# Tile 1's q and k over SyncE's ring with GpSimd casts, so that GpSimd's ring starts with the weights, and a new cost model in the planner

**Chip, cores, metric.** One core of one Trainium2 chip. The metric is device time in microseconds (us), lower is better; a time is the median of several runs. All times compared below are of undisturbed runs; the few runs that came in the second, slower state (over 1.5% above the fastest: four of the kernel before, one of before_tail3) are left out. They still spread: the 39 undisturbed runs of before, on several chips, go from 238.07 to 240.68 us. Times inside a trace count from the start of its span.

## What is computed

```python
# q, k, v: (4, 8, 768, 64); is_retrieval: 8 flags; n_sink 4; window 64
scores = np.matmul(q, k.transpose(0, 1, 3, 2)) / 8
mask   = causal for flagged heads, else causal & (sink | in_window)
a      = softmax(where(mask, scores, -1e9))
x      = np.matmul(a, v) -> (3072 tokens, 512)
h      = x @ w_in              # 512 x 2048
g      = h - np.tanh(h)
out    = g @ w_out             # 2048 x 512, fp32
```

## The kernel before

The 3072 tokens go in 12 tiles of 256. For each tile the kernel makes scores, exp, the product with v, x, its transpose xT, the first layer (`ph`), g (`gt`) and the second layer (`po`). A planner, `Plan`, takes all operations with estimated costs, simulates five engines and two DMA rings, and emits the program in the order in which its simulated clock started them. Two facts matter below: the order on each engine is fixed at build time, so an engine waits in order; and a changed cost or load in the head shifts the simulated clock, and so can reorder **everything** after it.

```python
class Plan:
    ...
    def run(self):
        ...
            _, ns, _, _, dma, _, port, _ = self.ops[i]
            self.start[i] = t
            order.append(i)
            free[e] = t + max(ns - self.OVERLAP[e], 40)
            ...
            for u in followers[i]:
                ready[u] = max(ready[u], t + ns)
            ...
            if dma:
                packets, each = dma
                rings["POOL" if e == "POOL" else "SP"].append(
                    [i, t + ns + (1200 if e == "POOL" else 300), each, packets * each / 16]
                )
        ...
        for i in order:
            self.ops[i][2]()
...
        def paired(nm, t):              # q or k in runs of 512 B, two tokens of a head
            return nm != "v" and t == 0
        ...                             # other fp32 loads: runs of 256 B
        def load_cast(t, w_after=(), names="qkv"):
            ...                         # GpSimd's DMA reads fp32 and writes fp16: no cast needed
                        nc.gpsimd.dma_start(
                            out=o, in_=src[b, :, s0 : s0 + 128, :].rearrange("h p d -> p h d")
                        )
...
        for half in range(2):           # tile 0 over SyncE's ring, in halves of the heads
            load(0, "qk", (half,))
            load(0, "v", (half,))
...
        cast_qk(0, (("ACT", "ACT"), ("ACT", "DVE")), (0,))
        load_cast(1, [("rv", 0, "v", 0, 1)], "qk")     # tile 1: four casting loads on GpSimd's ring
        if first:
            load_w_in(*W_IN[0], ())                    # then the first quarter of w_in
            load_cast(1, (), "v")
        ...
        if first:
            load_w_in(*W_IN[1], ())
            load_w_in(*W_IN[2], ())
            scale_v(0, "POOL")
            load_w_in(*W_IN[3], ())
            load_w_out(0, ())
            ...                         # tile 2 and the other quarters of w_out
```

## Time and profile before

| | before |
|---|---|
| time, median of 3 | 238.31 us (238.22 to 238.36) |
| span of the profiled run | 236.7 us |
| first matmul, last matmul start | 6.01, 231.54 us |
| quarters of w_in land | 17.05, 23.67, 26.36, 28.98 us |
| quarters of w_out land | 31.41, 37.32, 41.70, 44.36 us |
| last store issued, landed, end of span | 232.36, 234.73, 236.74 us |

TensorE (PE) carries the kernel. A useful measure for it, worked out from the trace's matmul records, is the **loss by time T**: T less the work begun by then, where a matmul counts as the median distance to the next one of its kind (a 128-row, 256-column matmul of the first layer 0.109 us, one of 512 columns in the second 0.216 us, and so on). All kernels here do 205.6 us of such work. In before the loss is 15.9 us by 28, 19.5 by 60, 23.5 by 140 and 26.0 by 220: from 60 us to the end it still grows by 6.5. The prediction, which is quoted below, shows the other lines.

### The profile page before, as it was taken

What the parts mean: (1) busy time and instruction counts of PE and PEld (TensorE: products, weight loads), DVE (VectorE), ACT (ScalarE), POOL (GpSimd) and SP (SyncE); (2) the same over time, 40 slices, a digit from 0 to 9 for tenths busy, and PEclk for the clock granted to TensorE, in tenths of its full rate; (3) what the DMA queues carried; (4) which work ended last, traced back from release to release, by engine and by line L of the source; (5) the groups of instructions that cost most, each with busy time, mean ns of one, the idle gap of its engine ahead of it and who ended that gap; (6) DMA issues with size and microseconds to landing.
All of it is one profiled execution on the core that took longest, in us unless ns stands there. A gap on an engine that the chain in (4) does not pass through costs nothing. (4 is left out here: it accounts for less than half of the span.)

```text
span 236.7 us, 5895 instructions
## 1 busy us (share of the span) xinstructions
PE 221.5 (94%) x2220; PEld 157.8 (67%) x2220; DVE 139.0 (59%) x343; ACT 143.6 (61%) x221; POOL 90.5 (38%) x218
## 2 busy tenths in 40 slices
PE   0889899999999999999999999999999999999991
PEld 0346687756776777777676777776776777777661
DVE  1856665864488657767666655667766546443300
ACT  3668677884588387466686649537759464444320
POOL 5999420089818068480814904606300000000000
PEclk9999999999999999999999999999999999999999
DMA  5999999999997999979989695998712101310121
GB/s 128 209 140 172 204 181 204 197 228 224 206 225 182 151 248 184 227 153 206 239 168 214 136 186 130 186 171 179 134 47 66 38 31 47 90 38 9 44 89 51
DMA packets 108130, 35.29 MB, mean 149 GB/s; under 512 B 100290, under 2 KB 104642, under 8 KB 108098
## 3 DMA queue, kind: packets, MB, share of 16 engines
q1 hardware_dynamic: 92642, 28.98, 60.5%
q0 software_dynamic: 15168, 5.77, 20.7%
q8 instruction: 18, 0.29, 0.5%
q10 hardware_dynamic: 288, 0.14, 0.2%
q14 instruction: 14, 0.11, 0.2%
HBM read 27.27 MB, written 6.29 MB: 142 GB/s over the span
## 5 line engine op out<-in xcount | busy, mean ns | idle before, releaser
L1135 PE MATMUL ph<-xT,win 128*128 128x256 f16 x768 | 101.7, 273 | 0.6 <-DMA win<-in_moe_w_in_dram 0.3
L1194 PE MATMUL po<-wout,gt 128*128 128x512 f16 (+1 forms) x400 | 98.0, 371 | 0.3 <-ACT ot L1170 0.3
L1148 ACT ACTIVATE th<-ph 128x512 f32<-128x512 f32 x96 | 57.6, 601 | 59.6 <-PE ph L1135 58.2
L1155 DVE SCALAR_TENSOR_TENSOR gt<-th,ph 128x512 f16<-128x512 f32 x96 | 65.4, 684 | 44.9 <-ACT th L1148 44.4
L1135 PEld LDWEIGHTS <-win 128*128 128x128 f16 x768 | 80.0, 114 | 13.0 <-issue 1.9
L961 ACT ACTIVATE pt<-sc 128x1024 f16<-128x1024 f32 (+1 forms) x78 | 68.5, 926 | 11.4 <-PE sc L941 10.9
L1194 PEld LDWEIGHTS <-gt 128*128 128x128 f16 x400 | 36.4, 98 | 24.6 <-issue 0.9
L680 POOL CAST t<-raw_rqk 128x256 f16 x72 | 28.5, 440 | 63.3 <-DMA raw_rqk<-in_k_dram 48.1
L1030 PEld LDWEIGHTS <-pt 128*128 128x128 f16 x552 | 25.9, 98 | 10.4 <-issue 0.9
L1030 PE MATMUL av<-v,pt 128*128 128x65 f16 x304 | 26.0, 195 | 0.1
L941 PE MATMUL sc<-qk 64*128 64x128 f16 (+1 forms) x412 | 23.8, 240 | 1.7 <-DVE qk L826 1.7
L941 PEld LDWEIGHTS <-qk 64*128 64x128 f16 x412 | 13.7, 94 | 13.5 <-issue 8.9
L675 POOL CAST v<-raw_rv 128x128 f16 x72 | 21.1, 335 | 4.2 <-DMA raw_rv<-in_v_dram 4.2
L1060 DVE TENSOR_TENSOR x16t<-av,rinv 128x128 f32 x72 | 20.8, 289 | 2.3 <-DVE rinv L1050 0.3
L1030 PE MATMUL av<-vf,pt 128*128 128x65 f16 x248 | 19.6, 193 | 0.0
L1170 ACT ACTIVATE ot<-po 128x512 f32<-128x512 f32 (+1 forms) x24 | 14.3, 596 | 8.5 <-PE po L1194 8.4
L996 DVE TENSOR_TENSOR pt<-pt,m 128x1024 f16<-128x1024 f16 x16 | 12.3, 768 | 8.0 <-ACT pt L961 8.0
L1050 DVE RECIPROCAL rinv<-av 128x4 f32<-128x4 f32 x48 | 8.6, 179 | 13.4 <-PE av L1030 13.4
L986 DVE TENSOR_TENSOR pt<-pt,mS 128x512 f16<-128x512 f16 x24 | 9.8, 449 | 6.7 <-ACT pt L961 6.7
L843 PEld LDWEIGHTS <-t 128*128 128x128 f16 x48 | 3.9, 107 | 8.9 <-ACT t L644 6.8
L523 DVE TENSOR_SCALAR m<-A,thr 128x512 f16<-128x512 f16 x16 | 7.4, 501 | 1.7 <-PE sc L928 1.2
L751 POOL TENSOR_TENSOR vf<-v,rflagr 128x260 f16<-128x260 f16 x12 | 7.5, 634 | 0.0
(95 smaller groups left out, 90.8 us busy)
## 6 DMA issues: line engine op xcount, KB each, us to landing
out_dram<-ot SPq DMA_DIRECT2D x23, 256.0 KB, 2.3
raw_rqk<-in_q_dram SPq DMA_DIRECT2D x20, 256.0 KB, 4.7
raw_rqk<-in_k_dram SPq DMA_DIRECT2D x20, 256.0 KB, 4.5
raw_rv<-in_v_dram SPq DMA_DIRECT2D x18, 256.0 KB, 4.4
win<-in_moe_w_in_dram POOLq DMA_DIRECT2D x4, 512.0 KB, 8.8
wout<-in_moe_w_out_dram POOLq DMA_DIRECT2D x4, 512.0 KB, 12.4
raw_rv<-in_v_dram SPq DMA_DIRECT2D x4, 128.0 KB, 4.7
t<-in_q_dram POOLq DMA_DIRECT2D x4, 128.0 KB, 9.5
```

The costliest lines, as they stand in the source:

```text
L675: nc.gpsimd.tensor_copy(out=v1s[b]()[:, lo : lo + NB, rank : rank + 1, 0:D], in_=raw_of("v", t)[:, :, at, :],)
L680: nc.gpsimd.tensor_copy(out=t16[t % 2][:, :, :, rank : rank + 1, :], in_=raws["rqk", t][0]()[:, :, :, at, :],)
L941: nc.tensor.matmul(out=sc()[:, hh, o : o + nb * 128].rearrange("p (i c) -> p i c", c=128), lhsT=ks.rearrange("p i c -> p (i c)")[p_, jb * ...
L961: lambda pt=pt, gi=gi, wid=wid, sc=sc: nc.scalar.activation(out=pt()[:, :, 512 * gi : 512 * gi + wid], in_=sc()[:, :, 0:wid], func=AF.Exp, ...
L996: nc.vector.tensor_mul(out=pv, in0=pv, in1=m4[:, h0 : h0 + 2, 256:512].unsqueeze(2).to_broadcast([128, 2, 2, 256]),)
L1030: nc.tensor.matmul(out=av()[:, i, hh, :], lhsT=pt()[:, hh, co : co + 128], rhs=vv, start=(jb == first_jb), stop=(jb == qb),)
L1060: nc.vector.tensor_mul(out=x16s[t]()[:, :, at, :], in0=av()[:, :, hh : hh + 1, 0:D], in1=rinv()[:, :, hh : hh + 1].unsqueeze(3).to_broadca ...
L1135: nc.tensor.matmul(out=ph()[:, j, :], lhsT=w()[:, cb, c0 + fb % 4 : c0 + 512 : 4], rhs=xTs[t]()[:, cb, :], start=(cb == 0), stop=(cb == HP ...
L1148: lambda: nc.scalar.activation(out=th()[:], in_=ph()[:], func=AF.Tanh, scale=1.0 / XS),
L1155: lambda: nc.vector.scalar_tensor_tensor(out=gts[t]()[:, u * FU : (u + 1) * FU, :], in0=th()[:], scalar=-XS, in1=ph()[:], op0=ALU.mult, op ...
L1170: nc.scalar.activation(out=ot()[:, c0:c1], in_=po()[:, c0:c1], func=AF.Copy, scale=1.0 / XS)
L1194: nc.tensor.matmul(out=po()[:, c0:c1], lhsT=gts[t]()[:, f, ts * 128 : ts * 128 + 128], rhs=w_out_t[f // 4]()[:, f % 4, c0:c1], start=(f == ...
```

## The change

Intent: GpSimd's ring should have w_in sooner. So q and k of tile 1 move to SyncE's ring, uncast, in 512 B runs behind tile 0's data, and GpSimd casts them; its first DMA is now a quarter of w_in. The planner's cost model is also made to fit the chip: half clock for TensorE before 15 us, later landings of the first loads on SyncE's ring, and an issue that follows another on GpSimd's ring can be planned a little sooner.

```diff
@@ class Plan @@
-            if k[0] in self.PSUM:
+            if isinstance(k, tuple) and k[0] in self.PSUM:
@@
+            if e == "PE" and t < 15000:
+                ns *= 2
@@
-                ready[u] = max(ready[u], t + ns)
+                ready[u] = max(ready[u], free[e])
@@
-                    [i, t + ns + (1200 if e == "POOL" else 300), each, packets * each / 16]
+                    [i, t + ns + (1200 if e == "POOL" else 1000 if t < 6000 else 400), each, packets * each / 16]
@@
-            return nm != "v" and t == 0
+            return nm != "v" and t < 2 and (first or not t)
@@ the load of is_retrieval
-                "ACT", 400,
+                "ACT", 1150,
@@ (tile 0's six loads are written out in the order that the loop gave; not shown)
@@
         cast_qk(0, (("ACT", "ACT"), ("ACT", "DVE")), (0,))
-        load_cast(1, [("rv", 0, "v", 0, 1)], "qk")
         if first:
-            load_w_in(*W_IN[0], ())
+            load(1, "qk", (0,))
+            load(1, "qk", (1,))
+            cast_qk(1, (("POOL", "POOL"), ("POOL", "POOL")))
+        else:
+            load_cast(1, [("rv", 0, "v", 0, 1)], "qk")
+        cast_v(0, ("POOL", "POOL"), (0,))
+        cast_v(0, ("POOL", "POOL"), (1,))
+        if first:
+            load_w_in(*W_IN[0], raw_keys("q", 0, 1))
             load_cast(1, (), "v")
@@ (the two cast_v(0, ...) lines further down go; a list of first-layer transposes is kept and not used; not shown)
```

> **What bounds the kernel now.** I read the page's table of busy time and the slices first, then busy time by stretch, then the waits of TensorE, then the timeline of the stretches in which TensorE is not full, and last the landings of the head's DMAs.
>
> ```profile
> PE 221.5 (94%) x2220; PEld 157.8 (67%) x2220; DVE 139.0 (59%) x343; ACT 143.6 (61%) x221; POOL 90.5 (38%) x218
> ...
> 6.00:15.00 9.00, 8.12 (x56) 3.85 (x57) 6.21 (x16) 6.00 (x11) 8.77 (x12) 1.00 1.62 179
> 15.00:19.00 4.00, 3.00 (x43) 1.80 (x42) 3.23 (x12) 2.94 (x7) 4.00 (x6) 1.00 1.50 138
> 19.00:22.00 3.00, 3.00 (x38) 2.44 (x39) 1.36 (x4) 2.79 (x4) 3.00 (x4) 1.00 1.18 182
> 22.00:28.00 6.00, 4.78 (x59) 3.17 (x56) 4.25 (x11) 3.92 (x8) 3.79 (x5) 1.00 1.23 213
> 28.00:36.00 8.00, 7.97 (x98) 6.91 (x96) 5.01 (x11) 5.86 (x12) 1.97 (x3) 1.00 1.79 178
> 36.00:60.00 24.00, 23.05 (x267) 16.40 (x266) 14.69 (x49) 16.77 (x25) 11.57 (x30) 1.00 1.17 215
> 60.00:100.00 40.00, 39.73 (x435) 28.88 (x434) 28.26 (x68) 28.09 (x41) 21.64 (x57) 1.00 1.06 205
> 100.00:200.00 100.00, 100.00 (x1019) 71.75 (x1017) 63.50 (x151) 63.28 (x95) 32.71 (x91) 1.00 0.69 138
> ```
>
> The columns of a stretch are its bounds, its length, and busy time of PE, PEld, DVE, ACT and POOL. From 60 us on TensorE is all but full, so the kernel is bound by TensorE, and a change of the head is worth only what it lets TensorE do earlier. Before 60 us its idle time is 6.00 (nothing has landed and been cast), 0.88 in 6 to 15, 1.00 in 15 to 19, nil in 19 to 22, 1.22 in 22 to 28, 0.03 in 28 to 36 and 0.95 in 36 to 60: 4.1 us after its first matmul. The end (the last evacuation starts at 231.91, the span ends at 236.7) is not touched.
>
> Who ends these waits, and what stands around the longest two:
>
> ```profile
> PE xp L1108 <- DVE x L1074: 1.1, 3, 0.6
> PE sc L941 <- DVE qk L826: 0.7, 1, 0.7
> PE ph L1135 <- DMA win<-in_moe_w_in_dram: 0.3, 1, 0.3
> ...
> 15.20 0.28 PE L843 MATMUL tp4q<-ident,t 128*128 128x128 f16 x2
> 18.93 1.06 PE L1135 MATMUL ph<-xT,win 128*128 128x256 f16 x8
> 23.72 0.63 PE L1135 MATMUL ph<-xT,win 128*128 128x256 f16 x4 [0.30 <-DMA win<-in_moe_w_in_dram]
> 26.65 0.89 POOL L378 DMA_DIRECT2D v<-in_v_dram  x1 [1.75 <-DMA win<-in_moe_w_in_dram]
> 35.82 9.16 SPq L328 DMA_DIRECT2D raw_rqk<-in_k_dram  x2
> ```
>
> The first three are waits (us, times, longest), the others timeline rows (start, length). tp4q is the first work of tile 1; L1135 is the first layer on tile 0. The row at 23.72 is the key: the second quarter of w_in came just in time, 0.30 us late. Landing times of the trace say the same of the others: the quarters landed at 17.05, 23.67, 26.36 and 28.98, and L1135's groups on tile 0 start at 18.93, 20.69, 23.72, 25.37, 27.30 and 29.42. So in 22 to 28 us tile 0's first layer follows the arrival of weights, though only 0.3 us is booked as a wait for a DMA: a TensorE whose order was planned for these arrivals shows thin work, not one long wait. Counting columns at full clock (columns divided by 2.4, my reckoning), TensorE did 4.2 us of work in those 6 us, a loss of about 1.8. POOL, too, waits there for an old transfer to land before it may issue a new one.
>
> **What the skill says, and whether this trace agrees.** (1) TensorE: Matmul & The Clock Gate, Part 1, "What's actually happening": the array starts at half clock and is let go after a busy window of about 3.4 us. Agrees in kind: the clock's records start at 14.95 us, and a 128x128 transpose takes about 300 ns before and 219 after. So 6 to 15 us runs at half clock with TensorE 90% busy, and little can be pulled into it. (2) DMA: Bandwidth & Descriptors, "Queues, rings and completion order": the engines take packets in turn from the rings that have work. Agrees: in 39 to 41 us, when POOL's ring carried w_out and SP's the next q and k, the trace has 56 and 48 packets of the one against 55 and 48 of the other in each us; SP moved only 14 and 12 KB in them. (3) The same page, Specifications: 512 B are needed for line rate. The halves of q and k of tile 0, which go in such pairs, land some 0.95 us apart (256 KB each, 270 KB/us), and the casting loads of tile 1's q and k moved about 150 KB/us of half-size output, that is 300 KB/us read: here the longer packets gain nothing. (4) GPSIMD Engine Reference, 4.1: operations with one input run at about line rate. Agrees: a 128x512 cast took 0.61 us on POOL, 0.58 on DVE and 0.62 on ACT.
>
> **The change part by part.**
> Tile 0's six half loads keep their order on SP's ring; the rewritten calls list what the loop listed. First work stays at 6.0 us: nothing gained.
> Removed: four casting issues of q and k of tile 1 on POOL, 1.10 + 0.89 + 0.88 + 0.88 = 3.75 us of POOL. Added: four casts of 128x512 at 0.61, 2.44 us. POOL gains 1.3 us and is not the bound, so nothing by itself.
> Moved: the first w_in quarter goes first on POOL's ring, after the second half of tile 0's q has landed (8.28 before). I expect its issue at about 9.0 and its first packets about 1.5 us later (the first POOL issue ended at 7.19, its packets start near 8.7), at 10.5. Alone a quarter takes 2.65 us, the step between landings.
> Tile 1's four half loads: SP's data for tile 0 ends at about 9.3 (1.2 us ahead of the landing at 10.52). At 1.86 ns a packet (0.95 us for 512) one half and a quarter of the next are through by 10.5. Then packets alternate with w_in's at 5.2 ns each (2.65 us for 512), 7.1 a pair: the remaining 380 of k's first half take 2.7 us. Adding 1.2 to land, first halves come at about 11.4 (q) and 14.4 (k), second ones, beside the casting v loads, at about 16.4 and 17.9. With a cast of 0.61 the first k is ready at 15.0. Before, all landed by 13.53, yet their first transposes ran at 15.2 (q) and 17.7 (k), the second halves' at 22.0 and 23.1. So the later arrival is still in time.
> Weights: all bytes up to the second quarter are the same, only the order differs, but the hole in the DMAs at 13 to 14 us (65 KB moved, against some 200) goes, as does the stretch of POOL's late issues. From 9.3: q and k 3.8, first quarter 2.65, v 2.0, second 2.65, plus 1.2 to land: 21.6. I expect quarters at about 15.3, 21.6, 24.3 and 27.0: the last three some 2 us earlier.
> What TensorE makes of it. In 22 to 28 us I expect back 1.0 of the lost 1.8: the groups of L1135 no longer follow the weights, while the in-order wait for DVE's copy (0.7) may stay. In 15 to 19 I take 0.3 of 1.0, since the first layer still needs tile 0's xT, whose last copy starts at 18.62. That the order planner now counts TensorE's half clock and later first landings is of use there. In 36 to 60 I take 0.3 of 0.95, because w_out and tiles 2 and 3 follow on the same rings and shift too. Sum 1.6: 238.3 - 1.6 = 236.7.
>
> **Rivals.** (a) Weights starve tile 1: by the packet turns of (2), SP's ring gets about 100 KB/us beside w_in. If w_in starts before tile 1's first halves are through, k lands past 17, POOL waits in order in its cast and issues the next weights late. For it: the 9.16 us in which SP was held in two issues. Against it: SP's loads are issued first. It would give 238.5 to 240. (b) Nothing: in 15 to 28 us the chain from matmul to exp to mask to av to x to xT, and DVE's order, set the pace, and weights were only 0.3 us late. For it: the three waits on DVE, 1.8 us against 0.3. It would give 237.9 to 238.4. (c) More: a denser start frees the clock one window of 3.4 us sooner, which saves half of it, 1.7 us, beside the 1.6: 235. Against it: nothing of tile 0 comes earlier.
>
> **Range and chances.** The middle is between (b) and a full recovery of the 3.2 us idle in 15 to 19, 22 to 28 and 36 to 60, which gives 235.1. Rival (a) sets the upper side. I take 235.2 to 238.4 for 8 in 10. Faster by over 2% means below 233.5, which needs more than all the idle time there is after the first matmul: 0.02. Slower by over 2% means above 243.1, which needs a stall that nothing shows: 0.01. Within: 0.97.
>
> **What would show the steps.** Right: w_in's second quarter lands before 22.5; TensorE idles under 0.6 us in 22 to 28; no wait for DMA win; first matmul still at 6.0 and clock at 15; total of TensorE's busy time within 1.5 us of before. Wrong: POOL casts of tile 1 that wait long for DMA raw_rqk, or transposes of tile 1 later than 17.7 with TensorE idle before them (a); quarters 2 us earlier with L1135 no denser (b); the clock's record beginning near 11.5 (c).

## The result, and the profile after

| | before | after |
|---|---|---|
| time, median | 238.34 us of 4 (238.22 to 238.83) | 238.47 us of 4 (237.85 to 238.73) |
| ratio after to before | | 0.9998 (0.9974 to 1.0022): the same |

A ratio is the mean time of one kernel's fast runs over that of the other's in the same rounds, so not quite the ratio of the medians quoted.

By 60 us the head, in sum, did what was hoped. Busy time by stretch in after, columns as in the prediction (xN counts instructions; the last three numbers are the granted clock, the busy share of the DMA engines and GB/s):

```profile
15.00:19.00 4.00, 3.50 (x48) 2.01 (x45) 3.66 (x11) 3.28 (x6) 4.00 (x7) 1.00 1.72 191
...
22.00:28.00 6.00, 5.24 (x64) 3.82 (x65) 3.76 (x11) 3.65 (x7) 2.60 (x4) 1.00 1.26 205
28.00:36.00 8.00, 7.38 (x90) 5.58 (x90) 4.77 (x11) 6.07 (x13) 3.16 (x4) 1.00 1.86 182
36.00:60.00 24.00, 24.00 (x283) 18.32 (x281) 15.63 (x49) 17.51 (x27) 13.22 (x38) 1.00 1.10 221
60.00:100.00 40.00, 39.51 (x434) 28.34 (x429) 27.15 (x66) 27.40 (x41) 21.69 (x58) 1.00 1.10 197
100.00:200.00 100.00, 99.75 (x1010) 71.48 (x1009) 64.89 (x151) 62.74 (x94) 31.33 (x83) 1.00 0.67 137
```

TensorE is fuller than before in 15 to 19 (3.50 for 3.00), 22 to 28 (5.24 for 4.78) and 36 to 60 (24.00 for 23.05), but thinner in 28 to 36, and also in 60 to 100 and 100 to 200, where nothing was meant to change. The waits of TensorE in after (total, times, longest; the 6.0 us before the first work and three shorter ones are left out):

```profile
PE po L1200 <- DMA wout<-in_moe_w_out_dram: 0.6, 2, 0.4
PE tp6k L848 <- ACT qk L829: 0.5, 1, 0.5
PE sc L934 <- ACT pt L967: 0.5, 1, 0.5
PE sc L947 <- DVE qk L831: 0.4, 1, 0.4
PE sc L947 <- DMA qk<-t: 0.4, 1, 0.4
```

The waits for w_in and for DVE's x are gone; waits for w_out and for a transpose by DMA (`qk<-t`) are new. The latter is in the middle of the body. TensorE's timeline in after (start, length, count, wait before it):

```profile
77.23 1.03 PE L1200 MATMUL po<-wout,gt 128*128 128x512 f16 x4
78.65 0.56 PE L947 MATMUL sc<-qk 64*128 64x256 f16 x10 [0.40 <-DMA qk<-t]
...
109.37 0.34 PE L947 MATMUL sc<-qk 64*128 64x128 f16 x4 [0.17 <-ACT pt L967]
```

What it waits for stands in SyncE's queue, in after:

```profile
70.60 2.54 SPq L1094 DMA_TRANSPOSE xT<-x16t  x2
73.23 3.47 SPq L703 DMA_TRANSPOSE qk<-t  x2
```

The two `qk<-t` transposes are issued one behind the other after two others, and the scores that need them are TensorE's next work. In both traces of before no scores wait for a transpose by DMA.

Both kernels were traced a second time on another chip (the last experiment). The ledger of the four traces, in us:

| | before | before, again | after | after, again |
|---|---|---|---|---|
| time of that run | 238.46 | 239.75 | 238.52 | 238.05 |
| loss by 28 | 15.92 | 15.81 | 14.98 | 14.86 |
| loss by 60 | 19.51 | 19.40 | 17.75 | 17.86 |
| loss by 110 | 22.37 | 22.34 | 21.61 | 21.39 |
| loss by 140 | 23.54 | 24.84 | 22.88 | 22.34 |
| last matmul starts | 231.54 | 232.87 | 230.90 | 230.43 |
| last store lands | 234.73 | 236.02 | 234.03 | 233.56 |
| landing to end of span | 2.005 | 2.010 | 2.776 | 2.776 |
| span | 236.7 | 238.0 | 236.8 | 236.3 |

Read the first trace of each: after leads by 1.76 us at 60, by only 0.63 at the last matmul, and not at all at the end. So 1.1 us go back in the body and 0.77 between the landing of the last store and the end. The experiments ask three things: what made the 1.76, what took back the 1.1, and what the 0.77 are.

### The profile page after: what moved, and what is told of

The parts are those of the page before. It is cut to its first block, busy times and chain, and to the rows that moved or that the text cites. A ratio compares the mean times of both kernels' runs of the same rounds, so it can differ in the third digit from the quotient of the medians.

```text
span 236.8 us, 5901 instructions
## 1 busy us (share of the span) xinstructions
PE 221.6 (94%) x2220; PEld 158.5 (67%) x2220; DVE 138.8 (59%) x343; ACT 142.7 (60%) x221; POOL 89.7 (38%) x218
## 3 DMA queue, kind: packets, MB, share of 16 engines
q0 software_dynamic: 11008, 5.24, 16.7%
## 5 line engine op out<-in xcount | busy, mean ns | idle before, releaser
L680 POOL CAST v<-raw_rv 128x128 f16 x72 | 20.4, 324 | 8.6 <-DMA raw_rv<-in_v_dram 8.6
L992 DVE TENSOR_TENSOR pt<-pt,mS 128x512 f16<-128x512 f16 x24 | 10.9, 495 | 7.2 <-ACT pt L967 7.2
L1002 DVE TENSOR_TENSOR pt<-pt,m 128x1024 f16<-128x1024 f16 x16 | 11.4, 713 | 6.2 <-ACT pt L967 6.1
L756 POOL TENSOR_TENSOR vf<-v,rflagr 128x260 f16<-128x260 f16 x12 | 8.1, 682 | 0.0
L934 PE MATMUL sc<-m,ident 128*128 128x384 f16 (+1 forms) x16 | 5.8, 452 | 0.5 <-ACT pt L967 0.5
```

What stands on the lines that cost most here:

```text
L680: nc.gpsimd.tensor_copy(out=v1s[b]()[:, lo : lo + NB, rank : rank + 1, 0:D], in_=raw_of("v", t)[:, :, at, :],)
L1002: nc.vector.tensor_mul(out=pv, in0=pv, in1=m4[:, h0 : h0 + 2, 256:512].unsqueeze(2).to_broadcast([128, 2, 2, 256]),)
```

## The experiments

My first theory: the moved loads make the advance; the planner's new order loses some of it again in the body; and the end is longer because SyncE's last store sits on another of its semaphores. Rivals: the advance comes from the better cost model; the weights do not matter; the stalls in the body are the run's noise.

### plan_only: the cost model alone

```diff
 (before.py)
+            if e == "PE" and t < 15000:
+                ns *= 2
-                ready[u] = max(ready[u], t + ns)
+                ready[u] = max(ready[u], free[e])
-                    (1200 if e == "POOL" else 300)
+                    (1200 if e == "POOL" else 1000 if t < 6000 else 400)
-                "ACT", 400,
+                "ACT", 1150,
```

(The mended dependence test, `isinstance`, is in it too; in route_only it is taken out.)

> The kernel before with the order planner's new model alone (TensorE at half speed before 15 us, later first landings, followers freed at the engine's overlap, the mended dependence test), loads as before. Measure: columns of matmuls begun by a time, divided by 2.4 columns per ns; by 60 us the kernel before had begun 45.06 us of such work and the changed one 47.15. Theory (the new order of the loads gives the advance): w_in quarters land at 17.0, 23.7, 26.4 and 29.0 as before and at most 45.6 us of work is begun by 60. Rival (the planner's better order gives the advance): at least 46.5 by 60. Time in either case 237.5 to 238.8.

Measured: 238.97 us (before on the same chip 239.14), ratio 0.9993 (0.9950 to 1.0036). The time is 0.2 above what was expected, and one expectation was missed clearly: the quarters of w_in landed at 15.88, 20.17, 24.13 and 26.20, as early as in after. The new order puts GpSimd's issues ahead of its casts (first casting load at 3.94 us, first quarter of w_in at 7.64; 6.09 and 11.13 in before); which of the model's edits does that was not tested. Yet the loss by 60 is 19.57, no advance at all. Busy time in plan_only:

```profile
6.00:15.00 9.00, 7.21 (x49) 3.52 (x50) 5.11 (x14) 5.14 (x9) 7.75 (x10) 1.00 1.69 203
...
22.00:28.00 6.00, 4.47 (x57) 3.52 (x55) 3.17 (x7) 4.39 (x9) 1.76 (x2) 1.00 1.38 200
```

6 to 15 is a microsecond thinner than in before (8.12): with the casting loads issued from 3.94 us beside tile 0's halves, tile 0's second k landed at 10.14 (9.26 in before) and its last v at 12.21 (10.52). So **early weights alone did not make the advance**: here they came with a later tile 0 and another order, and nothing was left by 60 us.

### route_only: the loads alone, old cost model

```diff
 (after.py)
-            if e == "PE" and t < 15000:
-                ns *= 2
-                ready[u] = max(ready[u], free[e])
+                ready[u] = max(ready[u], t + ns)
-                    (1200 if e == "POOL" else 1000 if t < 6000 else 400)
+                    (1200 if e == "POOL" else 300)
-                "ACT", 1150,
+                "ACT", 400,
```

> The changed kernel with the planner's old model: only the loads and casts are moved. Theory (loads give the advance): the last three quarters of w_in land about 2 us earlier than before (21.8, 24.0, 26.6), at least 46.5 us of work is begun by 60. Rival (planner): at most 45.6. If advances at 60 us are mostly given back later, whatever made them, the last matmul starts within 0.8 us of 231.5; if an advance is kept, 1.5 us sooner than 231.5 where 60 us shows 1.5.

Measured: 245.29 us (243.74 to 246.18), ratio 1.0263 (1.0215 to 1.0311), slower, though the weights landed as early as in after (16.03, 20.79, 23.30, 26.71). The theory that the loads alone make the advance falls. From the waits and the timeline of TensorE in route_only, and the row of granted clock on its page:

```profile
PE xp L1112 <- DVE x L1078: 2.4, 5, 1.2
```

```profile
19.78 0.39 PE L1112 MATMUL xp<-ident,x 128*128 128x128 f16 x2 [1.17 <-DVE x L1078]
...
20.86 2.62 PE L1139 MATMUL ph<-xT,win 128*128 128x256 f16 x12
```

```profile
PEclk9997999999999999999999999999999999999999
```

A likely reason: the old model plans tile 0 at full clock from the start, so TensorE's order puts the transposes of x sooner than DVE can deliver x. In the 3.41 us window from 16.39 to 19.81 TensorE then is busy only 47% of the time (by the union of its matmul records), and the record gives half clock in the next window, 19.81 to 23.22: twelve first-layer matmuls took 2.62 us there, where after's sixteen at full clock took 1.94 (start 19.00). Half of 3.41 is 1.7 us of work lost. The last matmul is 4.6 us later than before's, so the clock is not all of it; the rest was not taken apart. What route_only shows is that the loads do not pay under the old model, not what each costs.

### weights_late: one dependence changed

```diff
 (after.py)
-            load_w_in(*W_IN[0], raw_keys("q", 0, 1))
+            load_w_in(*W_IN[0], raw_keys("k", 1, 1))
```

> The changed kernel with the first quarter of w_in planned after the last half of tile 1's k instead of after tile 0's q: q and k of tile 1 go first again, but over SP. Theory (weights first gives the advance): quarters land at 23 or later from the second on, and at most 46 us of work is begun by 60. Rival (freeing POOL's ring of the four casting loads gives it, whatever the order): at least 46.8. Time 237.8 to 239.

Measured: 244.29 us, ratio 1.0219 (1.0173 to 1.0266): longer, though by the limit of 2% it stays unclear whether it counts as slower. The quarters landed at 21.10, 26.44, 28.98 and 31.59. The planner made a new order for this, and the clock fell to half again, from 26.43 to 29.84, after a window in which TensorE was 49% busy. So this run shows that late weights go with a longer time, but it mixes three things: the weights, the order and the clock. The run weights_delayed, below, separates them.

### tail7: the end of the program

SyncE waits at the end for eight DMA semaphores in turn, some 0.07 us each, and then goes through more waits and drains. Its DMAs, with ScalarE's two, use the eight in rotation: 125 of them in before, 129 in after, which issues four more on SyncE. So the last store fell on the fifth in before and on the first in after. What SyncE does from there, from the records of the two traces (start in us, instruction, semaphore; mine, cut):

```
before: 233.28 wait 100  233.38 101  233.47 103  233.55 104  | lands 234.73 |
        234.75 wait 106 (the last store's)  234.82 107  234.88 108  234.95 109
        twelve more 235.01 to 235.69, drain 235.76, end 236.74
after:  | lands 234.03 |
        234.05 wait 100 (the last store's)  234.15 101  234.23 103 ... 234.59 108
        twelve more 234.65 to 235.39, drain 235.80, end 236.81
```

In after all eight waits come behind the landing, and there is a hole of 0.4 us ahead of the drain. Seven one-element loads on SyncE, early, turn the rotation so that the last store gets the eighth semaphore:

```diff
 (after.py, behind load(1, "qk", (1,)))
+            for j in range(7):
+                op(
+                    "SP", 60,
+                    lambda j=j: nc.sync.dma_start(out=turn7[j][:], in_=q[0, 0, 0:1, j : j + 1]),
+                    w=[("turn", j)], dma=(1, 20.0),
+                )
```

> The changed kernel with seven more one-element loads on SP at about 10 us, which SP is free for: the semaphores of its DMAs are used in turn, so the last store gets the last of the eight that the end waits for in turn, where it now gets the first. From the landing of the last store to the end of the span it was 2.01 us before and 2.77 in the changed kernel. Theory (the order of these waits costs part of the 0.7 us by which the end grew): about 2.0 or less, the time 0.4 to 0.8 lower than the changed kernel's. Rival (the longer end is chance of one execution, or the clearing itself): 2.0 to 2.8 without a pattern, the time unchanged. The last matmul starts at 230.9 in both.

Measured: 237.65 us (236.58 to 238.14), ratio 0.9922 (0.9870 to 0.9975). Landing to end 1.700 us instead of 2.776; the head as in after (loss by 60 17.77), the stalls of the body as in after (0.96 at 78.94, 0.36 at 109.66). It was repeated on another chip:

> The kernel with the seven loads once more, beside its spliced form on one chip: last matmul at 230.9 to 231.2 with stalls of 0.5 to 1.0 at 78 to 79 and 0.5 at 109 to 110, 1.7 us from the last landing to the end, 0.990 to 0.997 of before. A second trace also tells how far one execution's stalls are chance.

Measured: 237.74 us of 6 (237.26 to 238.81), ratio 0.9939 (0.9880 to 0.9998), landing to end 1.700 again. For the end the expectation held twice; tail7_b's last matmul, at 230.71, was earlier than the 230.9 to 231.2 expected. Both ratios are under the 2% that counts as faster, and after did not run in the same rounds.

### before_tail3: the same for before

```diff
 (before.py, behind load_w_in(*W_IN[0], ()): the same loop)
+            for j in range(3):
```

> The kernel before with three one-element loads, which should give its last store the last of the eight semaphores that the end waits for; the order of all other instructions is the same. Theory (the order of these waits sets the end): from the last landing to the end of the span 1.7 us instead of 2.0, last matmul unchanged at 231.5, time 0.2 to 0.4 us lower, which the runs may not tell from noise. Rival (the end's length has another cause): 2.0 or without pattern.

Measured: 239.81 us of 5, ratio 1.0045 (0.9993 to 1.0096). Partly missed: the last store got the eighth semaphore and the waits behind it went, but the 0.4 us hole ahead of the drain came in, so landing to end is 2.256, not 1.7. And there was a stall that before's first trace had not shown:

```profile
110.94 1.50 PE L1136 MATMUL ph<-xT,win 128*128 128x256 f16 x12 [0.94 <-DMA xT<-x16t]
```

The hole is in every trace whose last store got the first semaphore, and in this one; it is in none of the other eight. Over all fifteen traces landing to end is 2.77 to 2.78 with the first semaphore (six), 1.92 to 2.01 with the fifth (four) and 1.70 with the eighth (four), before_tail3 being the exception. What opens the hole stays open.

### weights_delayed: weights late, order kept

Weights_late changed the order too. Here the order and all planned costs of after stay; only, a quarter of w_in that nobody uses is fetched ahead of the second one.

```diff
 (after.py, load_w_in)
+                if c0 == 512:
+                    nc.gpsimd.dma_start(
+                        out=extra[:],
+                        in_=moe_w_in[:, 0:512].rearrange("(cb p) f -> p cb f", p=128),
+                    )
```

> The changed kernel, its order kept, but POOL's ring fetches one more quarter of w_in (unused) before the second: the last three quarters land about 2.65 us later, near 24.4, 26.7 and 29.3, some 0.4 later than in the kernel before. Theory (the weights' earlier landing makes the advance): work begun by 28 us at most 14.2 (13.93 before, 15.14 changed), by 60 at most 45.4 (45.06 and 47.15). Rival (the advance is made by tile 1's q and k and by the new order): at least 14.8 and 46.6.

Measured: 241.53 us (241.49 to 241.83), ratio 1.0106 (1.0059 to 1.0153); quarters at 15.82, 24.03, 26.64 and 29.17, the last three about as late as in before. Loss by 60 is 20.12 (17.75 in after), and the last matmul starts at 233.66, 2.8 us after that of after. TensorE's waits:

```profile
PE po L1209 <- DMA wout<-in_moe_w_out_dram: 1.4, 2, 1.1
PE ph L1150 <- DMA win<-in_moe_w_in_dram: 1.0, 1, 1.0
```

So in after's order the early weights **are** needed, and their delay goes through to the end. The extra fetch delays all that follows on GpSimd's ring, w_out too (its quarters land at 31.57 to 44.53, 29.05 to 42.03 in after), and the longer waits are for w_out. From 36 to 60 us, though, the loss grows by only 1.9 (3.0 in before, 1.4 in after): most of the gain there comes with the order. With plan_only this says that neither early weights in another order nor this order with late weights made a gain by 60 us.

### packets512: loads of the later tiles in 512 B runs

The transposes that stall the body stand in SyncE's ring behind loads in 256 B runs. This kernel keeps after's order and reads q and k of the tiles from 3 on in 512 B runs of the same bytes. They land in other places, so its result is wrong on purpose (the record's check passed it all the same).

```diff
 (after.py, load)
+                                out=raw_of(nm, t)[:, i, h0 : h0 + nh, :].rearrange("p (h e) d -> p h (e d)", e=2),
+                                in_=src[b, 4 * i : 4 * i + 4, g * TT : (g + 1) * TT, :].rearrange("h (p e) d -> p h (e d)", e=2),
+                            ) if nm != "v" and ranked(t) else nc.sync.dma_start(
```

> The changed kernel, its order of instructions kept, but q and k of the second to fourth batch are loaded in 512 B runs (half as many packets, same bytes and buffers); the result is wrong on purpose. Theory (TensorE's stalls at 74, 78.6 and 109 come from loads, casts and transposes that are late on SP's ring): these stalls shrink to under 0.2 us each, the last matmul starts at 229.8 to 230.4 instead of 230.9. Rival (they are in the order of TensorE, ScalarE and VectorE): the stalls stay, last matmul at 230.7 to 231.1.

Measured: 238.36 us, ratio 0.9973 (0.9926 to 1.0020), last matmul at 230.41. At first this looked like half of the loss in the body regained: the stall near 78 us is down from 0.56 to 0.32 and one near 134 us is gone. But after's second trace, unedited, has its last matmul at 230.43 and the same stall at 0.32. So this run is **inconclusive**: what it moved is no more than one run of after differs from another. The stall near 109 us (0.36, waiting for an exp) stands in all of them.

### ahead3_tail7: loads of the later tiles planned one slot sooner

```diff
 (tail7)
-        AHEAD = 2.0
+        AHEAD = 3.0
```

> The changed kernel with the seven one-element loads and with loads, casts and transposes of the later batches planned 3 units ahead instead of 2. Theory (part of the head's advance is given back because TensorE waits for transposes that come over SP's ring, at 74, 78.6 and 109.4 us; planning them earlier takes the one at 109 away): no wait above 0.2 us at 105 to 112, the last matmul at 230.2 to 230.6 instead of 230.9; from the last landing to the end 1.7 us; time 0.985 to 0.993 of before. Rival (the stalls only move): last matmul at 230.8 or later, ratio that of the tail alone, 0.992 to 0.997.

Measured: 237.47 us (236.95 to 239.19), ratio 0.9930 (0.9893 to 0.9966): no better than tail7. Its profiled run was its slowest, and a stall of 1.45 us stood at 110.93, most of it a wait for `xT<-x16t`; the one near 79 was still there (0.74). The expectation, no wait at 105 to 112, was missed. One trace, of a long run, does not tell whether the planning or the run moved it.

### spliced and spliced_back: do the stalls belong to the order?

Spliced emits tail7's program as planned up to 40 us, and from there the operations in before's order. Spliced_back does the reverse: before's head and after's order.

```diff
 (Plan.run)
+        if self.gate is not None:
+            head = [i for i in order if i < self.gate or self.start[i] < 40000.0]
+            done = set(head)
+            order = head + [self.gate + k for k in OTHER if self.gate + k not in done]
```

> The kernel with the seven loads (tail7), its order kept up to 40 us of the plan; all that is left then follows in the order of the kernel before. Theory (the changed planner's order of the body gives the head's advance back: stalls of TensorE at 74, 78.9, 109.7 and 134 that stand at the same places of the order whatever the head does): columns begun by 60 us at least 46.5, the stall near 78.9 gone or under 0.5, none at 109; last matmul at 229.7 to 230.4 instead of 231.0; the span about 235.0 to 235.5. Rival (a head's advance is lost anyhow because the loads and transposes pace the body): last matmul at 230.8 or later.

> The reverse: the kernel before up to 40 us of its plan, then the changed kernel's order. Theory: stalls near 79 (0.5 to 1), 110 (0.5) and 135 (0.2) appear, the last matmul at 232.3 to 232.9 instead of 231.5. Rival: 231.3 to 231.8.

Measured: 240.14 and 240.62 us, ratios 1.0033 and 1.0035. Both expectations of the total were missed, and for one reason: the seam. In spliced:

```profile
40.12 1.91 PE L1226 MATMUL ph<-xT,win 128*128 128x256 f16 x16 [1.06 <-DVE gt L1246]
42.57 1.47 PE L1226 MATMUL ph<-xT,win 128*128 128x256 f16 x12 [0.54 <-DVE gt L1246]
...
112.16 1.50 PE L1226 MATMUL ph<-xT,win 128*128 128x256 f16 x12 [1.11 <-DMA xT<-x16t]
```

First-layer groups of two orders meet back to back and wait for DVE, so the head's advance is lost in 3 us. The totals say nothing of the body. The places of the stalls do. Spliced has none near 79 or 109.5, and has before's (0.46 at 76.3). Spliced_back has those of after, shifted by its 3 us:

```profile
77.53 1.06 PE L1219 MATMUL ph<-xT,win 128*128 128x256 f16 x8 [0.30 <-DMA xT<-x16t]
...
81.89 0.56 PE L1025 MATMUL sc<-qk 64*128 64x256 f16 x10 [0.46 <-DMA qk<-t]
```

So the stalls near 79 and 109 us belong to after's order of the body, not to its head.

Their cost can be read as well, since the seam lies before 60 us. From 60 to 110 us the loss grows by 2.9 to 3.1 in all four traces with before's order of the body (before, before_b, before_tail3, spliced), and by 3.4 to 4.1 in all seven with after's (after, after_b, tail7, tail7_b, packets512, weights_delayed, spliced_back), whichever head they have. So in this stretch after's order costs some 0.4 to 1.2 us more.

### before_b and after_b: both kernels again, unedited

Three kernels had now shown a stall of 1.1 to 1.5 us near 111 us (by the loss), two of them with before's order of the body. Was before's first trace a lucky one?

> The kernel before once more, unedited, for a second trace of it. If its order is really the better one in the body: only the stall of 0.46 near 75, the last matmul at 231.3 to 231.8. If its first trace was lucky there: a wait of about 1 us for the transpose of xT near 111, as in the two other kernels that keep its order in that stretch, and the last matmul at 232.3 to 232.7.

> The changed kernel once more, unedited, with its own five rounds. If its stalls belong to its order: 0.4 to 1.0 at 78 to 79 and 0.3 to 0.6 at 109 to 110, no stall above 1 us near 111, the last matmul at 230.5 to 231.2, 2.77 us from the last landing to the end; time within 0.5% of before on the same chip.

Measured: before_b 239.16 us of 6 (238.16 to 240.16), after_b 238.57 of 6 (237.95 to 239.24), against 238.56 for before in the same call: ratios 1.0018 (0.9984 to 1.0051) and 1.0001 (0.9974 to 1.0029). The traced run of before_b was one of the long ones (239.75). Its TensorE, then its SyncE, then its GpSimd:

```profile
109.77 0.34 PE L1030 MATMUL av<-v,pt 128*128 128x65 f16 x6
111.39 0.60 PE L1135 MATMUL ph<-xT,win 128*128 128x256 f16 x4 [1.27 <-DMA xT<-x16t]
```

```profile
102.34 1.26 SPq L698 DMA_TRANSPOSE qk<-t  x1
...
107.34 1.58 SPq L1088 DMA_TRANSPOSE xT<-x16t  x1
```

```profile
99.50 2.81 POOL L680 CAST t<-raw_rqk 128x256 f16 x8 [4.26 <-DMA raw_rv<-in_v_dram]
```

And the same three in the first trace of before, where the stall is missing:

```profile
110.05 1.48 PE L1135 MATMUL ph<-xT,win 128*128 128x256 f16 x12
```

```profile
101.21 1.26 SPq L698 DMA_TRANSPOSE qk<-t  x1
...
106.01 2.68 SPq L1088 DMA_TRANSPOSE xT<-x16t  x2
```

```profile
98.37 2.82 POOL L680 CAST t<-raw_rqk 128x256 f16 x8 [3.27 <-DMA raw_rqk<-in_k_dram]
```

A load of k lands 1.1 us later (99.35 for 98.22, issued 94.31 and 94.01), GpSimd casts later, SyncE's transposes queue 1.1 to 1.3 us later behind it, and TensorE stands for 1.4 us (by the loss). Before's order of the body is thus one load away from a stall; of the two traces the one without it took 238.46 us, the one with it 239.75. Three of the four traces with before's order have it, none of the seven with after's. How many of the untraced runs had it is not shown; ten of before's 39 undisturbed runs took over 239.5 us, and none of after's ten. After's body has small stalls always (0.56 and 0.32 at 79 us, 0.36 at 109 in both traces), so from 60 to 140 us its loss grows by 5.1 and 4.5, before's by 4.0 or, with the stall, 5.4. Noise is therefore part of the answer: what the body takes back is 1.1 us between the first traces and 0.5 between before's first and after's second; against before's second trace after gives nothing back in the body. After_b's stall near 79, 0.32, and its last matmul, 230.43, lie just below what was expected of them.

## Why the prediction was wrong

It said 236.7 us in a range of 235.2 to 238.4; the result was 238.47, just outside. That the verdict is "the same" it had right. By its own steps:

- **First work at 6.0 us, unchanged.** Right: 6.05.
- **Tile 1's q and k at 11.4, 14.4, 16.4 and 17.9, still in time.** Right: 11.28, 13.52, 15.94 and 17.50. No cast or transpose stood long for them, so rival (a) did not come.
- **Quarters of w_in at 15.3, 21.6, 24.3 and 27.0.** Right for three: 21.79, 24.01 and 26.61; the first came 1.35 us later than said. (Its reading that longer packets gain nothing compared two rings. On SyncE's ring alone a packet of 256 B took 18 ns and one of 512 B 27, medians of before's first 12 us.)
- **TensorE's gain of 0.3 + 1.0 + 0.3 = 1.6.** Right in sum, wrong in parts. The change of the loss, after against before: 0.12 gained until 15, 0.61 in 15 to 19, 0.19 lost in 19 to 22, 0.40 gained in 22 to 28, 0.76 lost in 28 to 36, 1.58 gained in 36 to 60; together 1.76. The loss in 28 to 36 is new waits for w_out (0.38 at 29.09 and 0.55 at 35.52 by the loss): w_out's second quarter lands at 35.48, earlier than before's 37.32, but after's order asks for it sooner still. The gain in 36 to 60 is mainly two waits of before for DVE, 0.44 at 37.32 and 0.82 at 47.88, that after's order does not have. That the sum fits is partly luck: in 22 to 28, where 1.0 was expected, 0.40 came, and TensorE still idled 0.76 there, over the 0.6 that the prediction named as its sign. The rows of these waits, two of before and one of after:

```profile
37.32 0.60 PE L1135 MATMUL ph<-xT,win 128*128 128x256 f16 x4 [0.27 <-DVE gt L1155]
47.88 0.34 PE L941 MATMUL sc<-qk 64*128 64x128 f16 x4 [0.63 <-DVE qk L826]
...
35.52 1.02 PE L1200 MATMUL po<-wout,gt 128*128 128x512 f16 x4 [0.39 <-DMA wout<-in_moe_w_out_dram]
```

- **The failing step: "a change of the head is worth only what it lets TensorE do earlier".** I took this to mean that the lead at 60 us is the lead at the end, since TensorE's row read 39.73 of 40 and 100.00 of 100. The step fails because the head's change is also a change of the planner's clock, and so gives the body another order. The lead at the last matmul was 0.63 us (1.11 in the second trace). The term that was missing is the body's own stalls: 1.1 us (0.5). From 60 to 110 us alone, where the spliced kernels show that the order is the cause, it is 1.0 (0.7).
- **The other failing step: "The end ... is not touched".** It is: landing of the last store to the end of the span went from 2.005 to 2.776 us in both pairs of traces, since four more DMAs on SyncE put the last store on the first of its eight end semaphores. That is +0.77, and tail7 showed that it can be had back with some change: 1.700.
- **Rivals.** (b), nothing, has the right time and the wrong reason: the first layer did get denser. (c), the clock one window sooner, did not come by the change: the record starts at 14.30 and 13.07 in after, at 14.95 and 10.51 in before, and the loss by 60 of before's two traces differs by 0.1 only.

The sum with what the runs put in place: -1.76 (head) + 1.13 (body) - 0.07 (last matmul to landing) + 0.77 (end) = +0.07 us, span 236.8 for 236.7; with after's second trace -1.65 + 0.54 - 0.07 + 0.77 = -0.41, span 236.3.

Not settled: what opens the 0.4 us hole ahead of the drain; what the order of the body costs on the average of runs, since after's costs more from 60 to 110 us and before's more near 111 in the runs that stall there; and why SyncE's transposes come too late near 79 us, since packets512 lies within after's own spread. The best version found is tail7: 237.65 and 237.74 us on two chips, some 0.8 us below after, which ran on other chips; the traces have 1.08 us less between landing and end. Its ratios to before (0.9922 and 0.9939) are helped a little by long runs of before in those rounds.

## What to carry to other kernels

When a scheduler orders the program, an edit of the head is an edit of the whole order: compare the stalls of the body, not only the head, and take no lead at a middle point for a lead at the end. In these runs weights that came early paid only where the order asked for them early, and the order planned for early weights cost more than it had gained when they were late. Look once at the last two microseconds: here the semaphore of the last store was worth about as much as the change of the head, and two traces of the same kernel tell how much of a difference is the run.

## What the Trainium skill lacked or had wrong

- TensorE: Matmul & The Clock Gate, Part 1, "What's actually happening", has the array go back to half clock after an idle window. Here it went back after windows in which it still was 47% (route_only, 16.39 to 19.81) and 49% busy (weights_late, 23.00 to 26.43), and stayed at full clock after windows of 57% (weights_delayed, 20.62 to 24.03), 64% (before_b, 20.75 to 24.16) and 70 to 72% (before, weights_late), counted in steps of 3.41 us from the first record of the clock. No page gives a busy share. The half-clock stretch was one window of 3.41 us each time, so about 1.7 us of work.
- No page has what the end of the program's own instructions costs: SyncE waited in turn for eight DMA semaphores, and from the landing of the last store to the end it took 1.70 to 2.78 us, mostly by which of them the last store had.
- DMA: Bandwidth & Descriptors, Specifications, asks for 512 B for line rate. That is not wrong here: SyncE's packets took 18 ns at 256 B and 27 at 512 B (medians, before's first 12 us). But the kernel's time does not show it: with 512 B runs for q and k of the later tiles 238.36 us, ratio 0.9973 (0.9926 to 1.0020), within the spread.
